# Chunk 0's state output as seven block products behind the last B projection, with its sums made by DMA

## The chip, the cores and the metric

The kernel runs on one core of a Trainium2 chip. The time is device microseconds of one execution. Five engines work side by side, each through its own list of instructions in order: TensorE (PE; its weight loads are PEld), VectorE (DVE), ScalarE (ACT), GpSimd (POOL) and SyncE (SP). SP, ACT and POOL also issue DMAs, each through a queue of its own. Waits between engines go by semaphores.

## What is computed

The input x has 2048 rows of 512. The output is x plus a state-space layer plus a gated feed-forward layer, both of the normalized x:

```python
xn = _layernorm(x, axis=-1)
# A: diagonal complex state, 512 wide, over 2048 steps
Bu = jnp.einsum("bld,pd->blp", x + 0j, B_bar)
for t in range(L):
    h = Lam_bar[None, :] * h + Bu[:, t, :]
y = 2.0 * jnp.einsum("blp,dp->bld", hseq, Cmat).real + x * Dskip[None, None, :]
# B: 1376 inner columns
g = _silu(x @ w_gate)
u = x @ w_up
return x + A(xn) + (g * u) @ w_down
```

All inputs and the output are bf16.

## The kernel before, in words

The rows go through in four chunks of 512 (c = 0 to 3). Everything that TensorE does for a chunk has one of four forms. `gateup_chunk` makes the 11 inner tiles of gate and up: two PSUM banks for a tile, evicted by ACT (silu at L511, a copy at L512), multiplied on DVE in pairs (L507). `bproj_chunk` makes the real and imaginary parts of the state's input (32 matmuls at L380, ACT evicts them at L382). `out_chunk` starts the output banks of a chunk's four row tiles from the inner products (`out_ffn`, L750) and adds the state's part (`out_ssm`, L762). The last two chunks' outputs are made together in `out_pair`.

Between B projection and state output stands DVE's part, `ssm_ops`: the input is rotated forward by a table of cosines and sines (six operations of 2048 columns at L390, L400 and L404), scanned (eight scans, L459), a carry is taken for the next chunk, and the scanned states are rotated back into the tile `wt`. For chunk 2's back rotation and chunk 3's forward rotation there is another form, `rotation_dma`: four operations on DVE (L420, L423), and the two sums are accumulating DMAs on POOL's queue (L426). It needs a table of negated sines, which `negate_table` (L411) writes on ACT.

The inner width is 10 tiles of 128 and one of 96. That last one is made once for two chunks at a time (`up_halves`, L539, half the columns of the array, and L550), multiplied (L527), moved by 12 small SP DMAs per chunk into 32-row pieces (`move_rows`, L188), and multiplied with four 32-row pieces side by side in the array (`out_rows`, L595). Their weights are loaded by four SP DMAs (`load_rows`, L182) into the place of half of the B weights.

`out_ssm_seven` (L644) makes the state output of a chunk with seven products of half blocks in place of eight: 56 matmuls of 256 columns in place of 32 of 512. It needs sums of the quarters of state (`state_sums`) and of the C weights (`weight_sums`). Before the change chunks 1 and 2 use it. A sum is a signed copy on ACT (L606) and an accumulating DMA on POOL (L610), one behind the other. In the end the results of the products are put together by DVE (L669).

Order around the change. The order of TensorE is written out at the end of the function: gate and up of chunk 1, B of chunk 2, all of chunk 0's output, gate and up of chunk 2, B of chunk 3, all of chunk 1's output, gate and up of chunk 3, `out_pair`. DVE's operations wait in a list, `backlog`. `pump` takes from it as many as the time given to it pays for, by costs written beside each operation; `need(tag)` empties it up to a tag; `multiply` puts the pair products between. `spend` issues the sums' operations between matmul groups. The C coefficients (`c_ops`: ACT scales at L363, DVE combines at L366) are in the list too, tag "cf". The normalization of chunks 2 and 3 takes its scale from POOL (L214), its offset from DVE (L217) and its rows from ACT (L235).

At the end, `out_pair` empties two of chunk 3's banks early into `part_end` and `jidx` (L734), which also frees the banks for `out_ssm_seven(2)`; chunk 3's state output (L762) follows, with DVE's last additions at L767. The skip term is prepared on DVE (L573 for four chunks, L576 adds x for the last), and stored by accumulating DMAs (L583). There are eight PSUM banks. Chunk 0's four output banks are held until its rows have been added in chunk 1's output.

Of the kernel before, what the change touches and what calls it, by code (L numbers as in the profile page):

```python
# [10 lines left out]
F32 = mybir.dt.float32  # L11
BF16 = mybir.dt.bfloat16
# [11 lines left out]
def kernel(  # L24
# [17 lines left out]
    nc = tc.nc  # L42
# [364 lines left out]
    neg_s16 = xnT[:, :, 0:CW]  # L407

    def negate_table():
        for q in range(NQ):  # L410
            nc.scalar.activation(out=neg_s16[:, q], in_=s16[:, q], func=ACT.Copy, scale=-1.0)  # L411

    def rotation_dma(src, dst, back):

        box = {}
        sines = (s16[:], neg_s16) if back else (neg_s16, s16[:])

        def side(i):
            t = box[i] = ssm.tile([128, NQ, CW], BF16, name="pm", bufs=3)
            V.tensor_tensor(out=t[:], in0=src()[:, i], in1=sines[i], op=ALU.mult)  # L420

        def main(i):
            V.tensor_tensor(out=dst()[:, i], in0=src()[:, i], in1=c16[:], op=ALU.mult)  # L423

        def join(i):
            nc.gpsimd.dma_start(out=dst()[:, i], in_=box[1 - i][:], accum_op=ALU.add)  # L426

        def f1():
            side(0)
        def f2():  # L430
            main(1) if back else main(0)
            if back:
                join(1)
        def f3():
            side(1)
            if not back:
                join(0)
        def f4():
            main(0) if back else main(1)
            join(0) if back else join(1)  # L440
        return [(1.15, f) for f in (f1, f2, f3, f4)]

    def ssm_ops(c):
# [9 lines left out]
        ops = (rotation_dma if c == 3 else rotation)(lambda: u_tiles[c], lambda: u_tiles[c], False)  # L453
# [27 lines left out]
        back = (rotation_dma if c == 2 else rotation)(g, wt, True)  # L481
# [4 lines left out]
    u_pair = {}  # L486
    products = []
# [12 lines left out]
    def u_tile(c, fi):  # L500
        if (c, fi // 2) not in u_pair:
            u_pair[c, fi // 2] = up_p.tile([128, 2, CW], BF16, name="u2")
        return u_pair[c, fi // 2]

    def product(c, fi):
        g, u = gu_tile(c)[:, fi - 1:fi + 1, :], u_tile(c, fi)[:]
        products.append(lambda: V.tensor_tensor(out=g, in0=g, in1=u, op=ALU.mult))  # L507
# [15 lines left out]
    def product_last(c):  # L523
        g, u = gu_last[c % 2][0:LB + LA, :], ul(c)[0:LB + LA, :]
        def mul():
            to = g if c == NCH - 1 else u
            V.tensor_tensor(out=to, in0=g, in1=u, op=ALU.mult)  # L527
            move_rows(c, to)
        products.append(mul)

    def up_halves():

        pss = []
        for c in range(0, NCH, 2):
            ps = bank()
            pss.append(ps)
            for k in range(KD):
                for i in range(2):
                    nc.tensor.matmul(ps[i * LB:(i + 1) * LB], lhsT=wu_last[:, k, :],  # L539
                                     rhs=xnT[:, k, (c + i) * CW:(c + i + 1) * CW], start=(k == 0), stop=(k == KD - 1))  # L540
        for c in range(NCH):
            i = c % 2
            nc.scalar.copy(out=ul(c)[0:LB, :], in_=pss[c // 2][i * LB:(i + 1) * LB])
        product_last(0)
        product_last(1)

    def gateup_last(c):
        ps = bank()
        for k in range(KD):
            nc.tensor.matmul(ps[:], lhsT=w_last[:, k, :], rhs=xnT[:, k, c * CW:(c + 1) * CW],  # L550
                             start=(k == 0), stop=(k == KD - 1))
        u = ul(c)
        nc.scalar.activation(out=gu_last[c % 2][0:LB + LA, :], in_=ps[0:LB + LA], func=ACT.Silu)
        nc.scalar.copy(out=u[LB:LB + LA, :], in_=ps[LB + LA:128])
        if c > 1:
            product_last(c)
# [18 lines left out]
    def skip_add():  # L575
        V.tensor_tensor(out=xn_end[:], in0=xn_end[:], in1=xall[:, NT - TPC:NT, :], op=ALU.add)  # L576
# [23 lines left out]
    neg_b22 = BT[:, 1, :, 0:HD]  # L600
    parts = {NT - 1: part_end, NT - 2: jidx}

    def signed_copy(out, in_, sign):

        for lo in range(0, NQ, 2):
            yield lambda lo=lo: nc.scalar.activation(out=out[:, lo:lo + 2], in_=in_[:, lo:lo + 2], func=ACT.Copy,  # L606
                                                     scale=sign)

    def added(out, in_):
        yield lambda: nc.gpsimd.dma_start(out=out, in_=in_, accum_op=ALU.add)  # L610

    def weight_sums():

        (b11, b12), (b21, b22) = BQ
        t1, t2, t3, t4 = TQ
        for out, in_, sign, to, add in ((t3, b12, -1.0, t3, b22), (t1, b11, -1.0, t1, b12), (t2, b11, 1.0, t2, t3),
                                        (t4, b22, -1.0, t4, t1)):
            yield from signed_copy(out, in_, sign)
            yield from added(to, add)
        yield from added(t4, b21)  # L620
# [6 lines left out]

    def state_sums(c):

        (a11, a12), (a21, a22) = state_quarters(c)  # L630
        if c == 1:
            s1, s2, s3 = (ssm.tile([128, NQ, HW], BF16, name="cm", bufs=3) for _ in range(3))
            s4 = jidx[:].bitcast(BF16).rearrange("p (q j) -> p q j", q=NQ)
        else:
            s1, s2, s3, s4 = ((wg_g, wu_g)[i // 2][2][:, :, (i % 2) * HD:(i % 2 + 1) * HD] for i in range(4))
        s_tiles[c] = (s1, s2, s3, s4)
        for out, in_, sign, to, add in ((s1, a21, 1.0, s1, a22), (s3, a21, -1.0, s3, a11), (s2, a11, -1.0, s2, s1),
                                        (s4, a12, -1.0, s4, s2)):
            yield from signed_copy(out, in_, sign)
            yield from added(to, add)  # L640
        if c == 1:
            yield from signed_copy(neg_b22, BQ[1][1], -1.0)

    def out_ssm_seven(c):  # L644
# [5 lines left out]
        space = flat(gu_tiles[c][:]).bitcast(F32).rearrange("p (s j) -> p s j", j=HD)  # L650
        high, low = (space[:, a:a + 4].rearrange("p (i h) j -> p i h j", h=2) for a in (2, 6))
        u2, five = high[:, :, 1], space[:, 0:2]
# [41 lines left out]
        if c == 1:  # L694
            step()
            step()
# [4 lines left out]
        product(a22, t4, at(1, 0), False, True)  # L701
# [3 lines left out]
        product(s4, neg_b22, at(0, 1), False, True)  # L705
        if c == 1:
            finish(1, high)
            finish(0, low)
            return pump(4 * 2 * NQ * 0.2163)
        finish(0, low)  # L710
        return lambda: finish(1, high)

    def out_pair(c):
# [4 lines left out]
        for op in state_sums(c):  # L718
            op()
        for n in range(c * TPC, (c + 2) * TPC):  # L720
            o = o_tiles[n][0]
# [8 lines left out]
        need(f"ssm{c}")  # L730
        need("skip")
# [232 lines left out]
    def spend(n, late=False):  # L964

        while n and sums:
            if sums[0] is None:
                if not late or any(item[3] == "ssm1" for item in backlog):
                    return
                sums[0:1] = state_sums(1)  # L970
            sums.pop(0)()
            n -= 1

    def bproj_chunk(c):
        need(f"ln{c}")
        for part in range(2):
            for q in range(NQ):
# [3 lines left out]
                spend(1, c == NCH - 1)  # L981
                if c == NCH - 1 and part == 1 and q == 0:
                    load_rows()

    def gateup_chunk(c):
        for fi in [FT - 1, *range(FT - 1)]:
# [3 lines left out]
            spend(2)  # L990

    def out_chunk(c):

        multiply(0)
        for n in range(c * TPC, (c + 1) * TPC):
            out_ffn(n)
            pump(FT * 0.2163)
            if c == 1:
                spend(4, True)
# [5 lines left out]
        if c == 1:  # L1005
# [6 lines left out]
        need("cf")  # L1012
        if c == 1:
            spend(99, True)
            return out_ssm_seven(c)
        for n in range(c * TPC, (c + 1) * TPC):
            out_ssm(n)
            pump(2 * NQ * 0.2163)
# [30 lines left out]
    queue("cf", c_ops())  # L1049
# [10 lines left out]
    fwd1, back1, _ = ssm_ops(1)  # L1060
    queue("ssm1", fwd1 + back1)
    gateup_chunk(1)
    nc.gpsimd.dma_start(out=dsk_bc[:], in_=A_Dskip.partition_broadcast(128))
    bproj_chunk(2)
    nc.sync.dma_start(out=out[0, 0:(NT - 2 * TPC) * 128, :], in_=A_x[0, 0:(NT - 2 * TPC) * 128, :])
# [7 lines left out]
    for c in range(NCH):  # L1073
        queue("skip", [(1.2, lambda c=c: skip_op(c)),
                       (0.0, lambda c=c: skip_store(c)) if c < NCH - 1 else (1.2, skip_add)])
# [34 lines left out]
```

## Time and profile before

| | |
|---|---|
| median of 3 runs | 176.83 us (176.67 to 177.0) |
| profiled execution | 177.04 us, its span 175.2 us |
| granted TensorE clock | 1.00 |
| PE busy | 171.7 us, 98% of the span |
| DVE busy | 161.1 us, 92% |
| ACT busy | 107.6 us, 61% |
| POOL busy | 45.9 us, 26% |
| L762 of chunk 0, 32 matmuls | 7.01 us |
| L657 of chunk 1, 56 matmuls | 6.22 us |
| accumulating DMAs of 512 KB (L426), issue to landing | 4.7 to 7.8 us |

A row of a timeline gives the start, the length, the engine, the line, the operation with what it writes and reads, and in brackets the idle time before it and what ended that. The chain of waits goes back from the last instruction to what released each step. Starts are microseconds from the span's start.

### The profile page before, as it was taken

The numbers are of one execution on the slowest core, as the hardware profiler recorded it, in microseconds if no ns is written. First come the engines' busy times: TensorE is split into PE (matmuls) and PEld (weight loads), VectorE is DVE, ScalarE is ACT, GpSimd is POOL, SyncE is SP. The second block draws the span as 40 slices with busy tenths as digits, with TensorE's granted clock in tenths as the row PEclk, the third lists the DMA queues.
The fourth block names the chain that finished last, engine by engine and source line by source line (L and its number), as shares of the span: only waits on it lengthen the run. The fifth ranks groups of instructions, "written<-read, shape, count | busy, mean of one in ns | idle before, by whom it ended". The sixth has DMA issues, their size and how long they took to land.

```text
span 175.2 us, 2790 instructions
## 1 busy us (share of the span) xinstructions
PE 171.7 (98%) x1002; PEld 88.4 (50%) x1002; DVE 161.1 (92%) x248; ACT 107.6 (61%) x204; POOL 45.9 (26%) x49
## 2 busy tenths in 40 slices
PE   8999999999999999999999999999999999999993
PEld 2977544444444444444444444468444444447743
DVE  4779998999999997999999999999999999995884
ACT  5487898868598669772998699052486691001100
POOL 6050120000400130000352224136544841211440
PEclk9999999999999999999999999999999999999999
DMA  6998496995332013700399449339898999955034
GB/s 170 294 170 226 91 250 117 362 230 121 77 76 30 0 30 75 254 4 11 43 105 120 60 51 194 61 60 136 139 156 153 157 175 192 122 60 60 0 105 139
DMA packets 38974, 21.36 MB, mean 122 GB/s; under 512 B 22016, under 2 KB 38144, under 8 KB 38944
## 3 DMA queue, kind: packets, MB, share of 16 engines
q0 software_dynamic: 9552, 8.26, 34.0%
q1 hardware_dynamic: 28016, 12.30, 31.1%
q10 hardware_dynamic: 1392, 0.62, 1.3%
q8 instruction: 8, 0.13, 0.3%
q14 instruction: 6, 0.05, 0.1%
HBM read 8.33 MB, written 4.19 MB: 71 GB/s over the span
## 4 chain that ended last, share of the span: by engine, by line
PE 98%; DVE 0%; issue 0%
PE ps L492 35%; PE ps L380 16%; PE ps L724 10%; PE ps L750 10%; PE ps L762 8%; PE ps L657 7%; PE ps L851 2%; PE ps L828 2%; PE ps L550 2%; PE ps L932 2%; PE ps L595 2%; PE ps L539 1%; PE ps L245 1%; DVE res L767 0%; PE ps L275 0%
## 5 line engine op out<-in xcount | busy, mean ns | idle before, releaser
L492 PE MATMUL ps<-xnT,wg 128*128 128x512 bf16 (+1 forms) x148 | 36.6, 373 | 0.0
L492 PE MATMUL ps<-xnT,wu 128*128 128x512 bf16 (+1 forms) x148 | 36.6, 373 | 0.0
L459 DVE TENSOR_TENSOR_SCAN g<-r_t,car,u 128x512 bf16<-128x512 f32 x24 | 28.7, 1264 | 0.0
L380 PE MATMUL ps<-xnT,BT 128*128 128x512 bf16 x128 | 28.3, 379 | 0.0
L511 ACT ACTIVATE guT<-ps 128x512 bf16<-128x512 f32 (+1 forms) x40 | 24.0, 599 | 5.4 <-PE ps L492 3.4
L512 ACT CAST u<-ps 128x512 bf16<-128x512 f32 (+1 forms) x40 | 23.3, 583 | 4.7 <-PE ps L492 4.5
L492 PEld LDWEIGHTS <-wu 128*128 128x128 bf16 x148 | 14.5, 98 | 16.6
L492 PEld LDWEIGHTS <-wg 128*128 128x128 bf16 x148 | 14.4, 98 | 16.5
L382 ACT CAST u<-ps 128x512 bf16<-128x512 f32 x32 | 18.2, 586 | 4.0 <-PE ps L380 3.9
L380 PEld LDWEIGHTS <-BT 128*128 128x128 bf16 x128 | 12.5, 98 | 14.9
L750 PE MATMUL ps<-wd_sb,guT 128*128 128x512 bf16 x80 | 17.6, 379 | 0.0
L724 PE MATMUL ps<-wd_sb,guT 128*128 128x512 bf16 x80 | 17.4, 379 | 0.0
L214 POOL TENSOR_TENSOR rstd<-ve,neg_half 128x2 f32<-128x2 f32 (+1 forms) x4 | 5.7, 1415 | 44.9 <-DVE ve L213 44.9
L762 PE MATMUL ps<-CF,wt 128*128 128x512 bf16 (+2 forms) x80 | 14.2, 336 | 0.0
L507 DVE TENSOR_TENSOR guT<-guT,u 128x1024 bf16<-128x1024 bf16 x20 | 13.4, 679 | 0.0
L724 PEld LDWEIGHTS <-guT 128*128 128x128 bf16 x80 | 7.8, 98 | 9.4
L750 PEld LDWEIGHTS <-guT 128*128 128x128 bf16 x80 | 7.8, 98 | 9.4
L205 DVE BATCH_NORM_STATS2 stats<-xall 128x6 f32<-128x512 bf16 x14 | 9.5, 679 | 2.0 <-DMA xall<-in_A_x_dram 2.0
L610 POOL DMA_DIRECT2D CT<-CF x3 | 3.9, 1300 | 27.1 <-ACT CT L606 23.6
L690 ACT COPY guT<-ps 128x512 f32<-128x512 f32 x2 | 1.2, 586 | 15.8 <-PE ps L657 15.8
L762 PEld LDWEIGHTS <-wt 128*128 128x128 bf16 x80 | 7.1, 98 | 6.9 <-issue 0.4
L459 DVE TENSOR_TENSOR_SCAN g<-r_t,u 128x512 bf16<-128x512 f32 x8 | 9.3, 1205 | 0.0
(168 smaller groups left out, 265.0 us busy)
## 6 DMA issues: line engine op xcount, KB each, us to landing
wd_sb<-in_B_w_down_dram SPq DMA_DIRECT2D x2, 640.0 KB, 8.7
xall<-in_A_x_dram SPq DMA_DIRECT2D x1, 1024.0 KB, 6.2
out_dram<-res POOLq DMA_DIRECT2D x8, 128.0 KB, 3.8
wt<-pm POOLq DMA_DIRECT2D x2, 512.0 KB, 5.4
u<-pm POOLq DMA_DIRECT2D x2, 512.0 KB, 6.2
out_dram<-xall POOLq DMA_DIRECT2D x2, 512.0 KB, 10.2
CT<-CF POOLq DMA_DIRECT2D x3, 256.0 KB, 4.3
gu_rows<-ul SPq DMA_DIRECT2D x36, 8.0 KB, 1.8
```

The source lines that it names most:

```text
L205: nc.vector.bn_stats(out=stats[:, n, :], in_=xall[:, n, :])
L380: nc.tensor.matmul(ps[:], lhsT=BT[:, part, k, q * 128:(q + 1) * 128], rhs=xnT[:, k, c * CW:(c + 1) * CW], start=(k == 0), stop=(k == KD - 1))
L382: nc.scalar.copy(out=u_tiles[c][:, part, q, :], in_=ps[:])
L459: V.tensor_tensor_scan(out=g()[:, part, q, :], data0=r_t[:, q:q + 1].to_broadcast([128, CW]), data1=u_tiles[c][:, part, q, :], initial=ini ...
L492: nc.tensor.matmul(ps[:fs, lo:hi], lhsT=wslice(groups, fi, k), rhs=xnT[:, k, c * CW + lo:c * CW + hi], start=(k == 0), stop=(k == KD - 1))
L507: products.append(lambda: V.tensor_tensor(out=g, in0=g, in1=u, op=ALU.mult))
L511: nc.scalar.activation(out=gu_tile(c)[:, fi, 0:hi], in_=psg[:, 0:hi], func=ACT.Silu)
L512: nc.scalar.copy(out=u_tile(c, fi)[:, fi % 2, 0:hi], in_=psu[:, 0:hi])
L657: nc.tensor.matmul(place(i), lhsT=a[:, q, i * 128:(i + 1) * 128], rhs=b[:, q, :], start=(start and q == 0), stop=(stop and q == NQ - 1))
L724: nc.tensor.matmul(o[:], lhsT=gu_tiles[k][:, fi, i * 128:(i + 1) * 128], rhs=wd_sb[:, fi, :], start=(fi == 0), stop=False)
L750: nc.tensor.matmul(o[:], lhsT=gu_tiles[c][:, fi, i * 128:(i + 1) * 128], rhs=wd_sb[:, fi, lo:hi], start=(fi == 0), stop=False)
L762: nc.tensor.matmul(o, lhsT=w_tiles[c][:, part, q, i * 128:(i + 1) * 128], rhs=CF[:, part, q, lo:hi], start=(fresh and part == 0 and q == 0 ...
```

## The change

Chunk 0's state output is taken out of `out_chunk(0)`. It is made by `out_ssm_seven(0)` behind the B projection of chunk 3, with chunk 0's 12 row products at its end. Its sums go into the places of chunk 0's and 1's normalized rows (`xnT`). For all three uses of the seven, the plain copies of the sums become DMAs on SP's or ACT's queue, negated copies stay on ACT, and the order of the sums is another one; the negated C quarter is no longer needed, since the sign has moved into the sums.

Chunk 0's back rotation and chunk 1's forward rotation take the DMA form. The negated sines are made during chunk 1's gate tiles and lie in `part_end` and `jidx`, so a multiplication with them is two operations of half width. The C coefficients stand behind chunk 1's forward rotation, and chunk 0's first sums between the first and the second coefficient.

The narrow tile's up part is made for chunks 0 and 1 before the B projection of chunk 2, and for 2 and 3 before that of chunk 3. The row moves of chunks 0 and 1 are issued on SP behind the copies for the sums; those of chunk 2 behind `out_ssm_seven(0)`; the weights of the rows behind the B projection of chunk 3. Chunk 0's and chunk 1's results both leave through DVE. The last skip addition becomes an accumulating DMA, the four skip products run in the order 3, 2, 0, 1, and the skip stores of chunks 0 and 1 are issued in `out_pair` behind chunk 2's state sums. The copy of x to the output rows of chunks 0 and 1 is issued some 13 us of PE work earlier. The four `u2` tiles of the pool become one tile of four places.

The diff, cut to its core:

```diff
-    neg_s16 = xnT[:, :, 0:CW]
+    neg_s16 = [t[:].bitcast(BF16).rearrange("p (q j) -> p q j", q=2) for t in (part_end, jidx)]
...
+            if i == (1 if back else 0):
+                for h, table in enumerate(neg_s16):
+                    q = slice(2 * h, 2 * h + 2)
+                    V.tensor_tensor(out=t[:, q], in0=src()[:, i, q], in1=table, op=ALU.mult)
...
-        ops = (rotation_dma if c == 3 else rotation)(lambda: u_tiles[c], lambda: u_tiles[c], False)
+        ops = (rotation_dma if c in (1, 3) else rotation)(lambda: u_tiles[c], lambda: u_tiles[c], False)
...
-        back = (rotation_dma if c == 2 else rotation)(g, wt, True)
+        back = (rotation_dma if c in (0, 2) else rotation)(g, wt, True)
...
     def skip_add():
-        V.tensor_tensor(out=xn_end[:], in0=xn_end[:], in1=xall[:, NT - TPC:NT, :], op=ALU.add)
+        nc.gpsimd.dma_start(out=xn_end[:], in_=xall[:, NT - TPC:NT, :], accum_op=ALU.add)
...
+        yield from copied(t4, b21, pieces=2)
+        yield from negated(t1, b11)
+        yield from added(t1, b12)
+        yield None
+        yield from negated(t2, b22)
+        yield from added(t2, t1)
+        yield from negated(t3, b12)
+        yield from added(t3, b22)
+        yield from added(t4, t2)
...
+        q = nc.scalar if c else nc.sync
+        yield from negated(s2, a22)
+        yield from copied(s4, a12, q)
+        yield from copied(s1, a21, q)
+        yield from negated(s3, a21)
+        yield from added(s3, a11)
+        yield from added(s1, a22)
+        yield None
+        yield from added(s2, s3)
+        yield from added(s4, s2)
...
-        product(s4, neg_b22, at(0, 1), False, True)
-        if c == 1:
-            finish(1, high)
+        product(s4, b22, at(0, 1), False, c > 0)
+        if c == 0:
+            for k in range(3):
+                out_rows(c, k)
+        between()
...
         if c == 0:
-            need("ln3")
-            up_halves()
-            negate_table()
-            multiply(0)
-        if c == 1:
-            for step in range(3):
-                for k in range(2):
-                    out_rows(k, step)
-            for n in range(TPC):
-                out_leave(n, o_tiles[n][0], opool.tile([128, D], BF16, name="res"))
+            need("cf")
+            sums.extend(leftover)
+            spend(0)
+            return
+        for k in range(3):
+            out_rows(c, k)
         need(f"ssm{c}")
...
-    queue("ssm1", fwd1 + back1)
+    queue("ssm1", fwd1[:turns])
...
+    queue("cf", cf[:1] + [(0.0, sums_begin)] + cf[1:] + [(0.0, sums_go_on)])
+    queue("ssm1", fwd1[turns:] + back1)
+    sums += negate_table()
     gateup_chunk(1)
+    nc.sync.dma_start(out=out[0, 0:(NT - 2 * TPC) * 128, :], in_=A_x[0, 0:(NT - 2 * TPC) * 128, :])
+    up_pair(0)
...
     out_chunk(0)
-    sums += [*weight_sums(), None]
+    move_rows(0, ul(0))
+    move_rows(1, ul(1))
     gateup_chunk(2)
+    up_pair(2)
+    product_last(2)
     bproj_chunk(3)
+    load_rows()
+    need("ssm1")
+    spend(99)
+    sums.extend(filter(None, state_sums(1)))
+    spend(99)
+    out_ssm_seven(0)
+    move_rows(2, ul(2))
```

More of the change, by code (lines that the diff above doesn't have):

```diff
@@ L527, in mul, with up_pair @@
             V.tensor_tensor(out=to, in0=g, in1=u, op=ALU.mult)
-            move_rows(c, to)
+            if c == NCH - 1:
+                move_rows(c, to)
         products.append(mul)
[L531 to L545, printed above, removed]
+    def up_pair(c):
+        ps = bank()
+        for k in range(KD):
+            for i in range(2):
+                nc.tensor.matmul(ps[i * LB:(i + 1) * LB], lhsT=wu_last[:, k, :],
+                                 rhs=xnT[:, k, (c + i) * CW:(c + i + 1) * CW], start=(k == 0), stop=(k == KD - 1))
+        for i in range(2):
+            nc.scalar.copy(out=ul(c + i)[0:LB, :], in_=ps[i * LB:(i + 1) * LB])
     def gateup_last(c):
@@ L599, with negated, copied @@
     TQ = [CT[:, i // 2, :, (i % 2) * HD:(i % 2 + 1) * HD] for i in range(4)]
-    neg_b22 = BT[:, 1, :, 0:HD]
     parts = {NT - 1: part_end, NT - 2: jidx}
-    def signed_copy(out, in_, sign):
+    def negated(out, in_):
         for lo in range(0, NQ, 2):
-            yield lambda lo=lo: nc.scalar.activation(out=out[:, lo:lo + 2], in_=in_[:, lo:lo + 2], func=ACT.Copy,
-                                                     scale=sign)
+            yield 1, lambda lo=lo: nc.scalar.activation(out=out[:, lo:lo + 2], in_=in_[:, lo:lo + 2], func=ACT.Copy,
+                                                        scale=-1.0)
+    def copied(out, in_, q=nc.sync, pieces=1):
+        n = NQ // pieces
+        for lo in range(0, NQ, n):
+            yield 0, lambda lo=lo: q.dma_start(out=out[:, lo:lo + n], in_=in_[:, lo:lo + n])
     def added(out, in_):
-        yield lambda: nc.gpsimd.dma_start(out=out, in_=in_, accum_op=ALU.add)
+        yield 0, lambda: nc.gpsimd.dma_start(out=out, in_=in_, accum_op=ALU.add)
     def weight_sums():
@@ L626, with halves, state_places @@
     s_tiles = {}
+    def halves(t, c):
+        return [t[:, :, c * CW + h * HW:c * CW + (h + 1) * HW] for h in range(2)]
+    def state_places(c):
+        if c == 0:
+            return halves(xnT, 0) + halves(xnT, 1)
+        if c == 1:
+            return [ssm.tile([128, NQ, HW], BF16, name="cm", bufs=3) for _ in range(2)] + halves(xnT, 2)
+        return halves(wg_g[2], 0) + halves(wu_g[2], 0)
     def state_sums(c):
         (a11, a12), (a21, a22) = state_quarters(c)
-        if c == 1:
[L632 to L640, printed above, removed]
-        if c == 1:
-            yield from signed_copy(neg_b22, BQ[1][1], -1.0)
+        s1, s2, s3, s4 = s_tiles[c] = [t[:] for t in state_places(c)]
+        q = nc.scalar if c else nc.sync
[8 more added lines that the diff above has]
+        yield from added(s4, s2)
     def out_ssm_seven(c):
@@ L649, in out_ssm_seven @@
         first = c * TPC
-        space = flat(gu_tiles[c][:]).bitcast(F32).rearrange("p (s j) -> p s j", j=HD)
-        high, low = (space[:, a:a + 4].rearrange("p (i h) j -> p i h j", h=2) for a in (2, 6))
-        u2, five = high[:, :, 1], space[:, 0:2]
+        if c == 0:
+            space = u_all[:].rearrange("p a b j -> p (a b j)").bitcast(F32).rearrange("p (s j) -> p s j", j=HD)
+            spots = (0, 4)
+            five = ssm.tile([128, D], F32, name="cm", bufs=3)[:].rearrange("p (i j) -> p i j", i=2)
+        else:
+            space = flat(gu_tiles[c][:]).bitcast(F32).rearrange("p (s j) -> p s j", j=HD)
+            spots = (2, 6)
+            five = space[:, 0:2]
+        high, low = (space[:, a:a + 4].rearrange("p (i h) j -> p i h j", h=2) for a in spots)
+        u2 = high[:, :, 1]
         def product(a, b, place, start, stop):
@@ L700, in out_ssm_seven @@
         skipped(0, low)
-        product(a22, t4, at(1, 0), False, True)
+        product(a22, t4, at(1, 0), False, c > 0)
+        between()
         add(high[:, :, 0], seven[:], u2)
@@ L717, in out_pair @@
             o_tiles[n] = [bank()]
-        for op in state_sums(c):
-            op()
         for n in range(c * TPC, (c + 2) * TPC):
+            if n == c * TPC + 1:
+                need("skip")
+                for _, op in filter(None, state_sums(c)):
+                    op()
+                skip_store(0)
+                skip_store(1)
             o = o_tiles[n][0]
@@ L729, in out_pair @@
                 out_rows(k, step)
-        need(f"ssm{c}")
-        need("skip")
         need(f"ssm{c + 1}")
@@ L962, with spend @@
     sums = []
[L964 to L972, printed above, removed]
+    def spend(n):
+        while sums and sums[0][0] <= n:
+            cost, op = sums.pop(0)
+            op()
+            n -= cost
     def bproj_chunk(c):
@@ L980, in bproj_chunk @@
                 multiply(0 if q else 1)
-                spend(1, c == NCH - 1)
-                if c == NCH - 1 and part == 1 and q == 0:
-                    load_rows()
+                spend(1)
     def gateup_chunk(c):
```

69 lines of the change are left out of this document (35 added, 34 removed).

## The prediction

> **What bounds the kernel now.** First the page's head, then its chain of waits in order of time, then busy time by stage.
>
> ```profile
> span 175.2 us, 2790 instructions
> ...
> PE 171.7 (98%) x1002; PEld 88.4 (50%) x1002; DVE 161.1 (92%) x248; ACT 107.6 (61%) x204; POOL 45.9 (26%) x49
> ```
>
> ```profile
> 72.24 1.85 PE ps L539 x16
> 74.09 7.01 PE ps L762 x32
> ...
> 99.23 6.91 PE ps L380 x32
> 106.14 8.63 PE ps L750 x40
> 114.77 1.41 PE ps L595 x24
> 116.17 6.22 PE ps L657 x56
> ...
> 159.20 6.36 PE ps L657 x56
> ```
>
> The chain (start, length, engine, line) never leaves TensorE until the last addition: work taken from PE is gained in full, as long as nothing else becomes late. What could is in the table by stage (window, its length, then busy time per engine):
>
> ```profile
> core 0: us, PE busy (x) PEld busy (x) DVE busy (x) ACT busy (x) POOL busy (x), PEclk, DMA share, GB/s
> 57.00:81.00 24.00, 24.00 (x120) 10.73 (x119) 22.39 (x30) 16.94 (x29) 1.92 (x1) 1.00 0.23 67
> 81.00:99.00 18.00, 18.00 (x85) 8.17 (x84) 17.93 (x24) 15.43 (x29) 6.42 (x5) 1.00 0.60 70
> 99.00:123.00 24.00, 24.00 (x158) 13.38 (x156) 23.79 (x30) 13.19 (x25) 8.56 (x9) 1.00 0.70 102
> 123.00:141.00 18.00, 18.00 (x85) 8.12 (x83) 17.79 (x21) 12.34 (x22) 9.92 (x10) 1.00 0.95 150
> 141.00:159.00 18.00, 18.00 (x102) 7.98 (x100) 17.70 (x17) 4.31 (x9) 5.11 (x4) 1.00 0.90 128
> ```
>
> From 57 to 159 us VectorE is busy 22.39 + 17.93 + 23.79 + 17.79 + 17.70 = 99.6 of 102 us. It is a second bound, just hidden. The two meet here:
>
> ```profile
> 157.58 1.23 DVE L404 TENSOR_TENSOR wt<-pm 128x2048 bf16<-128x2048 bf16 x1
> 159.25 0.69 DVE L734 TENSOR_TENSOR part_end<-ps,xn_end 128x512 f32<-128x512 f32 x1 [0.45 <-PE ps L595]
> ```
>
> L404 is the last operation of chunk 3's state; behind it L734 empties the PSUM bank that the second product of the last seven takes. DVE waited only 0.45 us for PE there, and PE took that bank at 159.20 + 0.86 = 160.06, when L734 had just ended. A DVE stream that comes later by more than about half a microsecond becomes the bound.
>
> **Part 1, TensorE.** Chunk 0's 32 full products (7.01) become 56 of half width (6.22): -0.79. The two groups that use part of the array are split, and each entry costs something: L539's 16 run two at a time, 8 x 8.63/40 = 1.73, so 0.12 of its 1.85 is entry; L595's 24 run four at a time, 6 x 0.216 = 1.29, entry 0.12 again; leaving L539 costs L762 7.01 - 6.91 = 0.10. One more L539 group: +0.22; one more L595 group +0.12, since what it leaves by takes the place of what is in the 6.22. Sum -0.45 (-0.35 to -0.6). If nothing waits, 177.04 (the profiled execution) becomes 176.6.
>
> **Part 2, the work of VectorE.** Two rotations, of chunk 0's state back and of chunk 1's input forward, go from six operations to four, the sums being made by accumulating DMAs: four operations less. The last skip addition becomes a DMA. Chunk 0's sums and results come onto DVE (before, ACT carried these results out).
>
> ```profile
> 120.62 0.68 DVE L669 TENSOR_TENSOR guT<-ps,guT 128x512 f32<-128x512 f32 x1
> ...
> 123.53 2.48 DVE L669 TENSOR_TENSOR res<-ps,guT 128x512 bf16<-128x512 f32 x4
> 125.93 1.21 DVE L420 TENSOR_TENSOR pm<-g,xnT 128x2048 bf16<-128x2048 bf16 x1
> ...
> 139.18 1.23 DVE L576 TENSOR_TENSOR xn_end<-xn_end,xall 128x2048 bf16<-128x2048 bf16 x1
> 140.32 0.68 DVE L507 TENSOR_TENSOR guT<-guT,u 128x1024 bf16<-128x1024 bf16 x1
> 140.92 2.45 DVE L459 TENSOR_TENSOR_SCAN g<-r_t,car,u 128x512 bf16<-128x512 f32 x2
> ```
>
> By distance between starts: chunk 1's four additions and four results are 125.93 - 120.62 = 5.3, and chunk 0's will be the same; a 2048-wide operation is 1.14 (139.18 to 140.32), or 1.25 behind the one it needs. So -4 x 1.2 - 1.15 + 5.3, and four multiplications that are cut in half add about 0.07 each: -0.4. Work alone relieves DVE a little. In this stretch it also waited:
>
> ```profile
> 62.80 0.16 DVE L217 SCALAR_TENSOR_TENSOR nb<-mv,rstd 128x4 f32<-128x4 f32 x1 [0.32 <-POOL rstd L214]
> ...
> 66.62 0.75 DVE L366 SCALAR_TENSOR_TENSOR CF<-CT,nc2im,cm 128x512 bf16<-128x512 bf16 x1
> ...
> 69.24 4.07 DVE L366 SCALAR_TENSOR_TENSOR CF<-CT,nc2im,cm 128x512 bf16<-128x512 bf16 x6 [0.56 <-ACT cm L363]
> 73.22 1.22 DVE L390 TENSOR_TENSOR pm<-u,c 128x2048 bf16<-128x2048 bf16 x1
> ```
>
> 0.4 with its reaction for the normalization's scale, and between the coefficients 73.22 - 66.62 less 8 x 0.66 (the last six: 3.98/6), 1.3; together 1.7. Without any wait the new stream would end chunk 3's state at 158.8 - 0.4 - 1.7 = 156.7. PE, 0.45 earlier, wants the bank at 159.6, so L734 must start by 158.9: **2.2 us of new waits are free**, each further one is paid in full.
>
> **Part 3, the new waits of VectorE.** The order of instructions shows four.
>
> (a) Chunk 3's scale. On POOL it now stands behind chunk 0's first join and the issue of the skip vector.
>
> ```profile
> 45.23 0.65 POOL L1063 DMA_DIRECT2D dsk_bc<-in_A_Dskip_dram  x1
> 60.85 1.92 POOL L214 TENSOR_TENSOR rstd<-ve,neg_half 128x4 f32<-128x4 f32 x1 [14.97 <-DVE ve L213]
> ```
>
> The first join's operation ends near 60.1; 0.3 of reaction (below), 0.85 and 0.65 put the scale at 61.9 to 63.8. DVE is there at 63.1: 0.7. It holds back the second join of chunk 0, to an issue at 65.4.
>
> (b) Coefficients. ACT negates chunk 0's quarters in front of five of the eight scalings that DVE's coefficients need, and two of these negations wait for that second join.
>
> ```profile
> 128.57 0.85 POOL L426 DMA_DIRECT2D wt<-pm x1 [0.58 <-DVE wt L423]
> 132.43 0.85 POOL L426 DMA_DIRECT2D u<-pm x1 [3.01 <-DVE pm L420]
> 133.69 0.85 POOL L426 DMA_DIRECT2D u<-pm x1 [0.41 <-DVE u L423]
> ```
>
> ```profile
> L426 POOL DMA_DIRECT2D wt<-pm x2: 846/850/853, 121.0 to 128.6; - x2
> L426 POOL DMA_DIRECT2D u<-pm x2: 846/847/848, 132.4 to 133.7; - x2
> ...
> DMA to landing us min/median/max: 4.7/5.4/7.8
> ```
>
> Asked one by one, these joins landed after 6.1 (121.0), 4.7 (128.57), 4.7 (132.43) and 7.8 us (133.69): 4.7 with an empty queue, up to 7.8 with others ahead or beside. So the second join is there at 70.1 to 72.
>
> ```profile
> 68.50 0.71 ACT L363 ACTIVATE cm<-CT,c2re 128x512 f32<-128x512 bf16 x1
> 69.11 0.71 ACT L363 ACTIVATE cm<-CT,nc2re 128x512 f32<-128x512 bf16 x1
> ...
> 75.55 2.19 ACT L411 ACTIVATE xnT<-s 128x512 bf16<-128x512 bf16 x4
> ```
>
> Two negations (2.19/4 = 0.55 each) and five scalings (0.61 from start to start) later the coefficients end at 75.8 to 77, against 75.3 by DVE's own eight times 0.66: 0.7.
>
> (c) Chunk 1's scan. DVE's first scan of part 1 needs the last of the two new input joins. Between that join's issue and the scan stand eight coefficients and a scan, 5.3 + 0.7 + 1.2 = 7.2 us; the join is the fourth in a row of 512 KB, with two copies of 256 KB beside: 7.8 or more, and half a microsecond until the waiter starts. 1.4 (0 to 3).
>
> (d) Chunk 3's scan. Before, the last join was issued at 133.69, landed at 141.5, and the second scan started at about 142.1: just in time. The change takes the skip addition (1.15) out of this gap, 8.4 becomes 7.25, and a join and four stores that were spread over 121 to 129 now stand 2.5 us closer ahead in the same queue. 7.8 and 0.5 less 7.25 is 1.05, with the queue 1.4 (0 to 3).
>
> Sum 4.2 (1.5 to 7.5). Less 2.2: PE waits 2.0 at the last seven products. **177.04 - 0.45 + 2.0 = 178.6**; the profiled execution was 0.2 over the median of the runs shown, 176.83, so on their scale 178.4.
>
> The Trainium skill (DMA: Bandwidth & Descriptors, Anatomy of one DMA) fits a DMA of this queue as 2.0 us plus bytes over 436 GB/s, an estimate of 3.2 us for 512 KB; by it (c) and (d) would be nothing and the time that of rival 1. The rows above speak against it: 4.7 at the least.
>
> **Parts that I cost at nothing, and their cover.**
>
> ```profile
> 78.33 26.18 SPq L188 DMA_DIRECT2D gu_rows<-ul x36
> ```
>
> ```profile
> CT<-CF POOLq DMA_DIRECT2D x3, 256.0 KB, 4.3
> ```
>
> Row moves: 24 issues on SP at 26.18/36 = 0.73 start behind the last coefficient, near 76, and end near 93.5; the four loads behind them wait for chunk 3's first B half (95.8) and land by 103; chunk 0's rows are used at 105.3. Accumulations of 256 KB at 4.3 and half a microsecond of reaction, one behind the other as the order has them, end the weight sums near 95, for products from 101 to 104, and chunk 1's fourth state sum near 118.7, for a product at 120.7. By the count of DVE's work above with (a) to (c), results leave chunk 1's banks from about 125.5 on, for gate tiles from 126.1 on. Four negations of the sine table move into chunk 1's gate tiles, where ACT had time between evictions. The skip stores move behind the last state sums, done near 168. If a cover is gone, PE waits for the difference. The thinnest is ACT at chunk 2's first gate tiles: the fifth bank must be free at 76.7, and by (b) ACT frees it at 76.1 to 77.3.
>
> **Rivals.**
> 1. All joins land under cover (waits up to 2.2). For it: two joins at 4.7, and DVE has 0.4 less work. Then PE alone counts: 176.6, or 176.4 on the medians' scale, faster. It decides at the free 2.2 us.
> 2. DVE keeps up, but ACT's wait for chunk 0's second join starves PE of banks in chunk 2's gate tiles: 0.6 (0 to 1.4) on top of rival 1, 177.0. It decides when that join lands later than 71.
> 3. Pile-up: with 512 KB joins and copies side by side (c) is 3 or more, chunk 1's results come too late for the gate tiles as well, and (a) to (d) reach 6.5: 177.04 - 0.45 + 4.3 = 180.9, or 180.7.
>
> **How the numbers follow.** Forecast 0.52 at 178.4, its own range 177.2 to 180; rival 1 0.25; rival 2 0.13; rival 3 0.10. Faster by over 0.2% (under 176.48, about what a measurement can tell) is rival 1: 0.25. Within 0.2% is most of rival 2: 0.13. Slower 0.62. The range takes in rival 1 and most of rival 3: 176.3 to 180.7.
>
> **What would show it.** In the changed profile: L734's addition starts right behind chunk 3's state with no wait for PE, and PE's second product of the last seven waits for it, 2 us; the second scans of chunks 1 and 3 wait for a DMA, 1 to 2 us each; the scale waits 0.7. The seven of chunk 0 takes 6.0 to 6.2 and starts without a wait. If these scans wait for nothing, I am wrong and rival 1 holds; if PE is idle near 77, rival 2.

## The result, and the profile after

The changed kernel takes **177.6 us** (median of 9 runs, 177.13 to 178.58), the kernel before 176.79 beside it (9 runs, 176.55 to 177.15): a ratio of 1.0053, 95% interval 1.0028 to 1.0078. It is slower by 0.5%, on the side that was forecast and inside the range, with about half of the forecast's loss (0.8 of 1.6 us). The reason is another one than forecast, so that sign and range came out right is luck. The profiled execution took 177.29 us. Ratios here and below leave out runs more than 1.5% above the fastest of the same kernel: one in the third experiment, two with chunk 1's rotation back.

The chain's shares by engine:

```profile
PE 38%; DVE 31%; SPq 15%; DMA 5%; ACT 5%; issue 3%; POOL 2%; DVEq 0%; ACTq 0%; POOLq 0%
```

Before, the chain stood on TensorE from the first microseconds on. Now it does so only from 106.17 us on; 15% of the span is SP's queue, and what stands ahead of that (VectorE's 31% above all) is the work up to the C coefficients, for whose copies SP waits. The chain of waits shows where (start, length, what):

```profile
77.97 1.36 SPq L188
...
99.84 0.53 SPq L182
...
101.36 4.77 DMA BT<-in_B_w_down_dram
106.17 0.80 PE ps L596 x9
```

Read it upwards: chunk 0's row products (L596) waited for the row weights of w_down (L182), whose four loads stand on SP behind all 24 row moves (L188). SP's own timeline gives the sizes, with the copies for the sums (L612) ahead of the moves, and TensorE's the wait:

```profile
75.06 2.86 SPq L612 DMA_DIRECT2D CT<-CF  x2
77.97 21.77 SPq L188 DMA_DIRECT2D gu_rows<-ul  x24
99.84 2.02 SPq L182 DMA_DIRECT2D BT<-in_B_w_down_dram  x4
```

```profile
105.25 0.39 PE L596 MATMUL ps<-BT,gu_rows 32*128 32x512 bf16 x3
106.17 0.80 PE L596 MATMUL ps<-BT,gu_rows 32*128 32x512 bf16 x9 [0.52 <-DMA BT<-in_B_w_down_dram]
106.91 8.81 PE L784 MATMUL ps<-wd_sb,guT 128*128 128x512 bf16 x40
115.64 0.83 PE L596 MATMUL ps<-BT,gu_rows 32*128 32x512 bf16 x12
116.40 0.83 PE L682 MATMUL ps<-CF,wt 128*128 128x256 bf16 x6
```

Chunk 1's twelve row products hold TensorE for 116.40 - 115.64 = 0.76 us; chunk 0's for 106.91 - 105.25 = 1.66. So the loads cost **0.90 us**, more than the 0.52 in brackets, which is one wait of several instructions.

VectorE, which the forecast had late, is not:

```profile
63.28 0.16 DVE L217 SCALAR_TENSOR_TENSOR nb<-mv,rstd 128x4 f32<-128x4 f32 x1 [0.30 <-POOL rstd L214]
71.93 3.40 DVE L366 SCALAR_TENSOR_TENSOR CF<-CT,nc2im,cm 128x512 bf16<-128x512 bf16 x5 [0.51 <-ACT cm L363]
77.37 8.34 DVE L464 TENSOR_TENSOR_SCAN g<-r_t,car,u 128x512 bf16<-128x512 f32 x7 [0.84 <-DMA u<-pm]
104.64 0.69 DVE L694 TENSOR_TENSOR u_all<-ps,u_all 128x512 f32<-128x512 f32 x1 [0.88 <-ACT u_all L715]
105.81 0.69 DVE L694 TENSOR_TENSOR u_all<-u_all,cm 128x512 f32<-128x512 f32 x1 [0.47 <-DVE u_all L694]
159.55 0.69 DVE L768 TENSOR_TENSOR part_end<-ps,xn_end 128x512 f32<-128x512 f32 x1 [0.42 <-PE ps L596]
```

These are all the waits that its timeline names between 56 and 160 us. At the last seven products (L768) it still waited 0.42 for TensorE, as before (0.45). The 0.88 at chunk 0's additions goes with the same loads: ACT, which had to copy out the product first, stood at a negation for chunk 1's sums until one of these loads had landed (the last one landed later, at 106.13). The negation uses nothing of them, and why it waits for them is not shown; with the loads earlier, in the first experiment, both waits are gone.

```profile
102.99 1.15 ACT L606 ACTIVATE xnT<-wt 128x512 bf16<-128x512 bf16 x2 [2.11 <-DMA BT<-in_B_w_down_dram]
```

So two theories stood against each other. **Theory A**: the loss is TensorE's wait for the row weights, because their loads are queued behind 24 row moves. **Theory B**, the one on record: VectorE is late at the last seven products, at least in the longer runs that no profile shows.

### The profile page after: what moved, and what is told of

It is laid out like the page before. It is cut to its first block, busy times and chain, and to the rows that moved or that the text cites. A ratio compares the mean times of both kernels' runs of the same rounds, so it can differ in the third digit from the quotient of the medians.

```text
span 175.5 us, 2872 instructions
## 1 busy us (share of the span) xinstructions
PE 171.4 (98%) x1026; PEld 89.8 (51%) x1026; DVE 160.2 (91%) x255; ACT 102.6 (58%) x194; POOL 55.1 (31%) x57
## 4 chain that ended last, share of the span: by engine, by line
PE 38%; DVE 31%; SPq 15%; DMA 5%; ACT 5%; issue 3%; POOL 2%; DVEq 0%; ACTq 0%; POOLq 0%
SPq L188 12%; PE ps L760 10%; PE ps L498 10%; PE ps L682 7%; DVE g L464 5%; PE ps L784 5%; DVE stats L205 5%; PE ps L796 4%; DVE pm L315 3%; DMA BT<-in_B_w_down_dram 3%; DVE guT L513 3%; DVE pm L390 3%; DMA xall<-in_A_x_dram 2%; PE ps L596 2%; ACT xn_end L235 2%
## 5 line engine op out<-in xcount | busy, mean ns | idle before, releaser
L518 ACT CAST u_all<-ps 128x512 bf16<-128x512 f32 (+1 forms) x40 | 23.3, 583 | 3.8 <-PE ps L498 3.6
L784 PE MATMUL ps<-wd_sb,guT 128*128 128x512 bf16 x80 | 17.6, 379 | 0.0
L513 DVE TENSOR_TENSOR guT<-guT,u_all 128x1024 bf16<-128x1024 bf16 x20 | 13.3, 678 | 0.0
L784 PEld LDWEIGHTS <-guT 128*128 128x128 bf16 x80 | 7.8, 98 | 9.6 <-issue 0.4
L431 POOL DMA_DIRECT2D wt<-pm x4 | 3.6, 908 | 23.8 <-DVE wt L428 16.8
L615 POOL DMA_DIRECT2D xnT<-wt x3 | 3.9, 1291 | 16.5 <-DMA CT<-CF 8.4
L711 POOL DMA_DIRECT2D out_dram<-res x8 | 8.0, 1837 | 0.0
```

Of the source, the lines that this page charges most:

```text
L518: nc.scalar.copy(out=u_tile(c, fi)[:, fi % 2, 0:hi], in_=psu[:, 0:hi])
L784: nc.tensor.matmul(o[:], lhsT=gu_tiles[c][:, fi, i * 128:(i + 1) * 128], rhs=wd_sb[:, fi, lo:hi], start=(fi == 0), stop=False)
```

## The experiments

### The loads ahead of chunk 1's moves

```
     move_rows(0, ul(0))
-    move_rows(1, ul(1))
...
     load_rows()
+    move_rows(1, ul(1))
     need("ssm1")
```

> The changed kernel, with the four loads of w_down's row weights issued on SP ahead of the twelve row moves of chunk 1 instead of behind them. Theory A (the loss is PE's wait for these loads, 0.52 us in the profiled execution and more in the longer ones, because they stand behind 24 row moves): the loads are issued as soon as PE has done with chunk 3's first B half, 95.8 to 97.5, land by 102, and the wait of 0.5 us ahead of chunk 0's row products is gone; 176.4 to 176.9, at or below the kernel before, and all runs within 0.5 us of each other. Theory B (the one on record: VectorE is late at the last seven products): nothing changes, 177.4 to 177.8.

Measured: 176.46 us (12 runs, 176.19 to 177.13) against 177.02, ratio 0.9975 (0.9961 to 0.9988). It beats the kernel before by 0.25%, where the change was 0.53% slower than it. SP's timeline, TensorE's and VectorE's in this kernel (its profiled run is the longest of its twelve; everything in it is about 0.7 us later from 55 us on):

```profile
78.55 11.69 SPq L188 DMA_DIRECT2D gu_rows<-ul  x12
96.29 1.85 SPq L182 DMA_DIRECT2D BT<-in_B_w_down_dram  x4
```

```profile
105.97 0.83 PE L596 MATMUL ps<-BT,gu_rows 32*128 32x512 bf16 x12
106.73 8.81 PE L784 MATMUL ps<-wd_sb,guT 128*128 128x512 bf16 x39
```

```profile
159.38 0.69 DVE L768 TENSOR_TENSOR part_end<-ps,xn_end 128x512 f32<-128x512 f32 x1 [0.59 <-PE ps L596]
```

The loads go out as soon as chunk 3's first B half has been read, the row products take 0.76 us, and nothing late takes the wait's place. Theory B alone would have shown no change. The runs do not lie within 0.5 us of each other as A expected; they spread over 0.9.

### Four moves twice

```
     move_rows(1, ul(1))
+    for p in range(4):
+        i, p = (3, p) if p < 3 else (2, 2)
+        nc.sync.dma_start(out=gu_rows[1][i * RT:(i + 1) * RT, p, :],
+                          in_=ul(1)[p * RT:(p + 1) * RT, i * 128:(i + 1) * 128])
```

> The changed kernel, with four of chunk 1's row moves issued a second time ahead of the loads of the row weights (the same bytes to the same place). Theory A: SP reaches the loads 4 x 0.9 = 3.6 us later and there is no slack behind it, so PE's wait ahead of chunk 0's row products grows from 0.5 to 4.1 us and the time from 177.6 to 181.2. Theory B: PE has slack there, since VectorE decides at the end; at most part of the 3.6 is seen, 177.6 to 180.

Measured: 181.57 us (4 runs, 180.34 to 182.79), ratio 1.0239 (1.0203 to 1.0274). The loads left 3.47 us later:

```profile
100.46 2.80 SPq L1108 DMA_DIRECT2D gu_rows<-ul  x4
103.31 1.99 SPq L182 DMA_DIRECT2D BT<-in_B_w_down_dram  x4
```

There is little slack behind SP's queue: an issue ahead of the loads is paid for on TensorE. From the start of the last of chunk 0's seven products to that of the FFN products it took 109.66 - 104.20 = 5.46 us in this profile, 106.91 - 104.29 = 2.62 in the change's, so 2.84 of the 3.47 are paid there, part of it at half clock. The profiled run is the longest of the four, and it lost 2.4 us more at the FFN products (11.18 us to their end, 8.73 in the change), by its clock; the last section says more. So the agreement of 181.57 with the 181.2 that A expected is partly chance: the one run whose granted clock stayed at 1.00 took 180.34.

### The last skip addition back on VectorE

```
     def skip_add():
-        nc.gpsimd.dma_start(out=xn_end[:], in_=xall[:, NT - TPC:NT, :], accum_op=ALU.add)
+        V.tensor_tensor(out=xn_end[:], in0=xn_end[:], in1=xall[:, NT - TPC:NT, :], op=ALU.add)
```

> The changed kernel, with the last skip addition back on VectorE (1.15 us of work there) instead of an accumulating DMA. Theory A: the 0.4 us that L768 waited for PE and 0.1 until PE takes the bank cover part of it, so 0.6 is seen: 178.2, with PE waiting 0.6 at its second product of the last seven. Theory B: VectorE is late already, so all of it is seen: 178.75 or more.

In the list of VectorE's operations it has its cost of 1.2 again. Measured: 178.4 us median of 6 runs (177.87 to 182.72), ratio 1.0078 (1.0056 to 1.0101) where the unaltered change has 1.0053; the profiled execution took 177.87, 0.58 more than 177.29. L768 now waits for nothing, and TensorE's second product of the last seven waits for it:

```profile
160.13 0.68 DVE L768 TENSOR_TENSOR part_end<-ps,xn_end 128x512 f32<-128x512 f32 x1
```

```profile
160.87 1.03 PE L682 MATMUL ps<-CF,wt 128*128 128x256 bf16 x8 [0.64 <-DVE part_end L768]
```

The first of these products began at 159.19, so the second came 1.68 us behind it, against 0.87 without a wait: 0.81 of some 1.2 us added are seen. (The spans differ by only 0.6, because the row products waited 0.3 less in this profile.) VectorE's room in the change is thus 0.4 to 0.5 us: the 0.42 that L768 waited, and less than 0.1 until TensorE takes the bank. This pair of rows is what the prediction expected of the change itself. The intervals of the two ratios overlap, so the size rests on the profiles.

### The moves issued where their products are made

```
-            if c == NCH - 1:
+            if c != 2:
                 move_rows(c, to)
...
-    move_rows(0, ul(0))
-    move_rows(1, ul(1))
```

> The changed kernel, with the 24 row moves of chunks 0 and 1 issued where their products are made, as before the change, so ahead of chunk 3's transposes and of the copies for the sums on SP instead of behind them. The products are there at 61.8, the moves then take SP from about 62 to 84. Theory A: the loads of the row weights are then in time (95.8 to 97.5), but chunk 3's transposes end near 91, just when TensorE wants them (0 to 1 us of waiting), and the copies near 97 instead of 78; the sums on POOL wait for these copies and end some 16 us later, 111 for products at 101 to 104, so PE waits about 7 us: 184 (181 to 186). Theory B: the same wait comes, less what VectorE was late by, 183. A rival by which the copies hold up nothing: 176.8.

Measured: 185.75 us (4 runs, 185.13 to 187.78), ratio 1.0518 (1.0471 to 1.0565), as A expected. SP, POOL and TensorE in the profiled run, the longest of the four:

```profile
61.78 21.76 SPq L188 DMA_DIRECT2D gu_rows<-ul  x24
...
90.61 1.29 SPq L612 DMA_DIRECT2D CT<-CF  x2
```

```profile
93.31 1.28 POOL L615 DMA_DIRECT2D xnT<-wt  x1 [20.11 <-DMA xnT<-wt]
```

```profile
108.48 4.59 PE L682 MATMUL ps<-CT,xnT 128*128 128x256 bf16 x24 [7.19 <-DMA CT<-CT]
114.79 1.03 PE L682 MATMUL ps<-CT,wt 128*128 128x256 bf16 x8 [1.71 <-DMA CT<-CT]
```

Moves ahead of the copies, the sums come 7 to 9 us late; moves behind them, the loads come 1 us late. The one queue cannot serve both, unless the moves are parted as in the first experiment.

### The change once more

No edit.

> The changed kernel once more, unaltered, so that it stands beside the others on the same chip. All theories: 177.3 to 177.9, 0.3 to 0.7% above the kernel before, with runs spread over more than 1 us. Theory A adds that PE waits between 0.5 and 2 us for the loads of the row weights, whichever run is profiled.

Measured: 177.79 us (6 runs, 177.34 to 178.71) against 176.81, ratio 1.0061 (1.004 to 1.0082). Its profiled execution took 177.71, 0.42 more than the first. TensorE there:

```profile
105.39 0.39 PE L596 MATMUL ps<-BT,gu_rows 32*128 32x512 bf16 x2
...
107.31 8.81 PE L784 MATMUL ps<-wd_sb,guT 128*128 128x512 bf16 x40
```

The row products hold it 107.31 - 105.39 = 1.92, so the wait is 1.16 here and 0.90 in the first profile. The longest runs of the change, 178.4 to 178.7, were not caught by a profile; that they have more of the same wait is argued, not shown.

### Chunk 0's full products again, with the loads ahead

The state output of chunk 0 as before the change, on top of the first experiment's order; chunk 0's sums are not made.

```
-    out_ssm_seven(0)
+    for n in range(TPC):
+        out_ssm(n)
+        pump(2 * NQ * 0.2163)
+    for k in range(3):
+        out_rows(0, k)
+    for n in range(TPC):
+        out_leave(n, o_tiles[n][0], opool.tile([128, D], BF16, name="res"))
```

> The changed kernel with the loads ahead of chunk 1's row moves (as in the first experiment), and chunk 0's state output as 32 full products again, its results carried out by ACT, without chunk 0's state sums. Theory A: nothing but PE's own work is left in the path, so it costs 7.01 - 6.22 less 0.1 at the entry, 0.7: 177.15 against 176.46. Rival C (the first experiment gained by the order of the moves, and the seven products bring nothing): 176.3 to 176.6, since VectorE has 5.3 us less. Both: the 6 transfers of these sums gone, a row move takes less than 0.9 us on SP, towards 0.73.

Measured: 177.23 us (12 runs), ratio 1.003 (1.0017 to 1.0044): 0.5% above the first experiment. Rival C falls. The moves are quicker, 8.62/12 = 0.72 us each against 11.69/12 = 0.97 in the first experiment:

```profile
75.19 8.62 SPq L188 DMA_DIRECT2D gu_rows<-ul  x12
```

TensorE's own account is cleanest from the start of the last group of gate and up of chunk 1 to the start of the last seven products. The two rows for, in this order, the kernel before, the change, the first experiment, and this one:

```profile
55.67 1.03 PE L492 MATMUL ps<-xnT,wu 128*128 128x512 bf16 x4
...
159.13 1.92 PE L657 MATMUL ps<-CF,wt 128*128 128x256 bf16 x16
```

```profile
55.43 1.03 PE L498 MATMUL ps<-xnT,wu 128*128 128x512 bf16 x4
...
159.43 1.92 PE L682 MATMUL ps<-CF,wt 128*128 128x256 bf16 x16
```

```profile
56.15 1.03 PE L498 MATMUL ps<-xnT,wu 128*128 128x512 bf16 x4
...
159.25 1.92 PE L682 MATMUL ps<-CF,wt 128*128 128x256 bf16 x16
```

```profile
55.26 1.03 PE L498 MATMUL ps<-xnT,wu 128*128 128x512 bf16 x4
...
159.16 1.92 PE L682 MATMUL ps<-CF,wt 128*128 128x256 bf16 x16
```

That is 103.46, 104.00, 103.10 and 103.90 us. The seven products save 103.90 - 103.10 = 0.80. The split groups cost 103.90 - 103.46 = 0.44. The change without its wait, 104.00 - 0.90, is 103.10, the same as in the first experiment, so in these profiles the wait is all that parts the two.

### The two new rotations back on VectorE, with the loads ahead

Chunk 1's input only, then also chunk 0's state:

```
-        ops = (rotation_dma if c in (1, 3) else rotation)(lambda: u_tiles[c], lambda: u_tiles[c], False)
+        ops = (rotation_dma if c == 3 else rotation)(lambda: u_tiles[c], lambda: u_tiles[c], False)
...
-        back = (rotation_dma if c in (0, 2) else rotation)(g, wt, True)
+        back = (rotation_dma if c == 2 else rotation)(g, wt, True)
```

> The changed kernel with the loads ahead of chunk 1's row moves, and the rotation of chunk 1's input with its sums on VectorE again. VectorE has two additions more, less two cuts of a multiplication, 2.3 us, and one wait less (the second scan's, 0.9). Theory A with a room of 0.6 at the last seven: 0.8 late, 177.25. Rival (VectorE still has the 2.2 us of room that the prediction gave it): 176.5.

> The changed kernel with the loads ahead of chunk 1's row moves, and both rotations (chunk 0's state, chunk 1's input) with their sums on VectorE again: four additions more, less four cuts, 4.5 us. Back come the second scan's wait (0.9) and that for the coefficients (up to 0.5). Theory A with a room of 0.6: 2.5 late, 179.0, with no wait of L768 for PE. Rival (2.2 us of room): 177.4.

Measured: 184.11 us (6 runs, 182.71 to 186.16), ratio 1.0388 (1.036 to 1.0417), and 185.0 us (5 runs, 184.77 to 185.85), ratio 1.0471 (1.045 to 1.0492). Both expectations missed by 6 to 7 us, because most of the loss is not at the last seven. With chunk 1's rotation on VectorE, first VectorE, then TensorE, in the profiled run, the longest of its six:

```profile
70.45 1.23 DVE L390 TENSOR_TENSOR pm<-u,s 128x2048 bf16<-128x2048 bf16 x1 [3.29 <-DMA wt<-pm]
...
75.37 5.38 DVE L366 SCALAR_TENSOR_TENSOR CF<-CT,nc2im,cm 128x512 bf16<-128x512 bf16 x8
```

```profile
75.85 1.03 PE L498 MATMUL ps<-xnT,wg 128*128 128x512 bf16 x4
80.64 1.87 PE L498 MATMUL ps<-xnT,wu 128*128 128x512 bf16 x4 [3.77 <-ACT ul L555]
```

The third product of that rotation needs a buffer that chunk 0's join still reads (3.29 us), so the coefficients start at 75.37 instead of 69.35. ACT's scalings for them wait too, the evictions of chunk 2's first gate bank queue behind these on ACT, and TensorE is left without a bank for 3.77 us. That is the mechanism and the place of the prediction's rival 2, reached by another cause. In the change itself ACT freed that bank at 75.42, and TensorE took it at 76.37. So in this order of operations chunk 0's rotation cannot take the DMA form alone without that wait. At the last seven TensorE waited 0.93 for L768 in this run, near the 0.8 that a room of 0.6 was expected to give. With both rotations back, the wait for ACT at the first place is 2.48 us, and VectorE is late at the last seven as well:

```profile
167.19 1.31 PE L682 MATMUL ps<-CF,wt 128*128 128x256 bf16 x8 [3.35 <-DVE part_end L768]
```

That is more than the 2.5 expected for this place with a room of 0.6, and far from the 0.9 or so that a room of 2.2 would leave. Since TensorE's first wait shifted everything between, neither of these two waits is a measurement of the room.

## Why the prediction was right in its sign and wrong in its reason

The forecast said that TensorE would gain 0.45 and then wait 2.0 us for VectorE at the last seven products. The gain came, that wait did not, and another wait, of 0.90 to 1.16 us at chunk 0's row products, made the kernel slower. That this landed on the forecast side and inside the range is luck.

- **TensorE's work, -0.45.** Held: -0.36 (103.10 against 103.46). The seven products gave 0.80 for the 0.79 forecast; the two split groups cost 0.44 instead of 0.34.
- **VectorE's work, -0.4.** A little more came off. Busy time from 57 us to the end of chunk 3's state (windows of before and after):

```profile
57.00:158.80 101.80, 101.80 (x539) 48.37 (x541) 99.61 (x116) 62.20 (x113) 31.93 (x29) 1.00 0.65 101
```

```profile
57.00:159.10 102.10, 101.58 (x562) 50.39 (x560) 98.51 (x122) 55.40 (x99) 38.68 (x37) 1.00 0.85 133
```

  99.61 became 98.51, -1.1. At 57 us the change was 0.25 further on in the same list of operations (the operation that began at 56.93 before began at 56.68), so -0.8 is the work.
- **VectorE's new waits, 4.2.** Mis-sized throughout: (a) 0.30 where 0.7 was forecast (0.32 before); (b) 0.51 for 0.7; (c) 0.84 for 1.4; (d) none for 1.4. Their sum is 1.65. The joins (L431) landed as taken from the rows of before:

```profile
DMA to landing us min/median/max: 4.8/5.3/7.4
```

  3.2 us, the estimate by the Trainium skill's fit (DMA: Bandwidth & Descriptors, Anatomy of one DMA), is below all of them, and scan (c) did wait. The idle time in those windows went from 2.2 to 3.6 us, 0.9 of it due to the loads.
- **"PE waits 2.0 at the last seven".** Fell: L768 waited for PE. VectorE ended chunk 3's state 0.32 us later than before (L404 begins at 157.90, before at 157.58), and TensorE came 0.30 later (159.43 and 159.13). The cause is the size of the sum above: 1.65 of new waits where 4.2 were forecast, against 2.2 that were free. In the change the waits at chunk 0's additions (0.88 and 0.47) come on top, but the loads made TensorE late as well; in the first experiment, where only the 0.47 is left, L768 waited 0.59 for TensorE. As to the joins, rival 1 was right: by themselves they cost nothing. With the loads out of the way the kernel is 0.56 us faster than the one before (176.46 against 177.02), where rival 1 had 0.45.
- **The step whose failure cost the time** stood among the covers costed at nothing: "Row moves: 24 issues on SP at 26.18/36 = 0.73 start behind the last coefficient, near 76, and end near 93.5; the four loads behind them [...] land by 103". They started at 77.97, since the two copies of 128 KB (L612) also hold SP for 2.86 us; they took 21.77/24 = 0.91 each; so they ended at 99.74, and the fourth load landed at 106.13. The rate of 0.73 had come from a stretch in which the DMA engines were far less busy:

```profile
78.00:105.00 27.00, 27.00 (x127) 12.26 (x126) 26.90 (x34) 20.89 (x40) 7.68 (x6) 1.00 0.53 63
```

```profile
78.00:99.80 21.80, 21.80 (x109) 9.94 (x107) 21.73 (x28) 17.36 (x33) 9.04 (x7) 1.00 0.98 131
```

  The column behind the granted clock (1.00) is the DMA share: 0.53 in the kernel before, 0.98 in the change, whose sums move through the same engines in that stretch. Without chunk 0's sums a move took 0.72 again. Single moves say the same: of the 36 before, the 26 issued while the engines were less than 0.9 busy held SP for 0.58 us on average, the other 10 for 0.90; of the 24 in the change it is 8 at 0.65 and 16 at 0.94. The mean share of a longer stretch is only a rough guide: with the moves at their products, 24 took 0.91 each at a mean share of 0.72. How the traffic slows an issue on SP is not shown. Late start 2.0 and slower moves 24 x 0.18 = 4.3 make 6.3 us, against a cover of 2.3 ahead of the loads (93.5 to 95.8) and 2.3 behind them (103 to 105.3): with these two terms the prediction's own sum would have given a wait of 1.7. It was 0.90 because the loads landed 6.3 us behind the first of their issues (99.84 to 106.13), where 7.2 had been allowed (95.8 to 103).
- **The other covers held.** The last products of chunk 0's and chunk 1's seven waited for no sum, no gate tile waited for a bank, and the seven of chunk 0 started without a wait, at 99.05, and ended at 105.25, 6.2 us.
- The loss is 0.36 gained and 0.90 to 1.16 lost: +0.54 and +0.80 for the two profiled runs, which lie 0.50 and 0.90 above the medians of the kernel before (176.79 and 176.81). The medians of the change lie 0.8 and 1.0 above them.

## What to carry to other kernels

When a change puts small DMAs on a queue, follow that queue to the last thing behind them with a deadline, and take the issue rate from a stretch whose DMA engines are as busy as they will be after the change (here 0.73 us a move was taken, and 0.91 came). A loss that hides a gain is found by moving one thing in the queue: one line moved turned a kernel 0.5% slower than before into one 0.25% faster. A cover is a number to be summed like any term, not a reason to cost a step at nothing.

## What the runs showed of the hardware

A wait of TensorE can cost more than itself. Each row below gives a window, its length and TensorE's busy time in it; the granted clock is the third column from the right. First the kernel with chunk 1's rotation back, around the wait of 3.77 us, then the one with both rotations back, around that of 2.48, then the one with four moves twice, ahead of its fall of the clock:

```profile
76.25:79.66 3.41, 0.62 (x3) 0.20 (x2) 3.41 (x6) 3.41 (x6) 2.10 (x2) 1.00 0.83 90
79.66:86.48 6.82, 5.84 (x14) 2.07 (x14) 6.82 (x7) 5.65 (x12) 2.59 (x2) 0.50 0.78 113
```

```profile
75.65:79.06 3.41, 0.93 (x5) 0.39 (x4) 3.41 (x7) 3.37 (x7) 1.26 (x1) 1.00 1.16 142
79.06:82.47 3.41, 3.41 (x9) 1.18 (x8) 3.41 (x3) 3.38 (x7) 1.00 (x2) 0.50 0.57 96
```

```profile
104.41:107.82 3.41, 1.94 (x11) 0.85 (x9) 0.02 (x1) 1.68 (x4) 0.23 (x1) 1.00 0.88 245
```

In the first the clock was 0.50 for 6.83 us, from 79.66 to 86.48, and a group of four products took 1.87 us instead of 1.03; in the second it was 0.50 for 3.41 us. The five falls between start and end of the work in these traces lasted 3.41 us (both in the kernel with both rotations back) or 6.83 us (four moves twice, the moves at their products, chunk 1's rotation back), so the clock changes in steps of 3.41 us; the stretches at full clock in these traces, 13.65 to 174.08 us long, are whole multiples of it too. Each time it came back at the end of the first such step in which TensorE was busy throughout. In the step ahead of a fall TensorE was busy for 0.93 us or less in four of the five, and for 1.94 of 3.41 us in the kernel with four moves twice, where no single wait was over 0.8 us. What counted there, the sum of the waits or the row products' small share of the array, no run here shows.

The Trainium skill (TensorE: Matmul & The Clock Gate, Part 1: The HAM clock gate) states half rate after an idle window of about 3.4 us, released after as long a busy one. The length of the steps and the release fit this; but the window was not wholly idle in four of the five falls, and a wait of 2.48 us was enough. In the kernel with four moves twice the times of the four runs go with it: 180.34 us at a mean granted clock of 1.00, 181.43 and 181.72 at 0.991, 182.79 at 0.981.

The waits of 0.90 and 1.16 us in the change left the clock at 1.00: the FFN products behind them (L784) took 8.81 us, as in the first experiment.
